# The inverse of the softmax sums moved from VectorE to GpSimd: top-k attention and a gated MLP in one kernel

## The chip, the cores and the metric

The kernel runs on one core of a Trainium2 chip. The metric is device time in microseconds. Engines are named as in the profile: PE is TensorE (PEld its weight loads), DVE is VectorE, ACT is ScalarE, POOL is GpSimd, SP is SyncE, which here issues nearly all DMAs.

## What is computed

Eight batches of eight heads, 576 rows of 64 numbers each. Of every row of scores only the 32 largest are kept; the rest get a weight of zero. Then an MLP with a sigmoid gate runs over the joined heads.

```python
scores = scale * np.matmul(q, k.transpose(0, 1, 3, 2))
kth = np.partition(scores, -top_k, axis=-1)[..., -top_k:-top_k + 1]
scores = np.where(scores >= kth, scores, -1000000000.0)
scores = scores - np.max(scores, axis=-1, keepdims=True)
attn = np.exp(scores)
attn = attn / (np.sum(attn, axis=-1, keepdims=True) + 1e-09)
x = np.matmul(attn, v)                 # heads joined: 4608 rows of 512
h = x @ w_in                           # 512 -> 2048
out = (h * (1.0 / (1.0 + np.exp(-1.702 * h)))) @ w_out
```

The change is about the division by the sum.

## The kernel before, in words

The attention is cut into 144 slots. A slot is 128 rows of scores for two heads: a tile of 128 x 2 x 576. Eighteen slots make a batch. The order of the instructions is written out by hand, slot by slot, and each engine works off its own instructions in that order.

In a slot n:

- `scores` (L328, PE) multiplies queries and keys into the only pair of score banks in PSUM.
- `copy_scores` (L339, ACT) copies them to `sc`, and `pair_up` (L349, DVE) takes the larger and the smaller of each two scores from the bank and the copy. Only then may PE write the next scores into the banks.
- `topk` (L375 MAX8 and L379 MATCH_REPLACE8, DVE) finds the 32 largest in four rounds of eight for each head, 14 steps in all.
- `bounds` (L393 `cut` and L394 `low`, POOL) makes the two bounds from the largest and the 32nd value.
- `mask` (L407, ACT) pushes scores below the cut far down, `exps` (L417, ACT) takes the exponentials into `pr` and their sum into `den`.
- `invert` (L426 or L428, and L430) adds 1e-9 to the two sums of every row (`some`) and takes their inverse (`rden`): 128 x 2 numbers.

What uses the inverse differs with the stage:

- In slots 0 to 10 (`slot`) `divide` (L437, POOL) multiplies the identity by it into two diagonals (`by`). PE turns the exponentials with these (`turn_main`, `turn_ends`, L457 and L460, one slot later), which divides them on the way; ACT copies the result to `pt` (L465). In these slots the weights are also brought in and rounded in pieces, by ACT (L155, L157, L159), DVE (L158) and POOL (L148, L151, L156). Between its other work PE runs filler products to stay warm (`stay_warm`, L174).
- From slot 11 on (`first_pair`, `filling_pair`, `steady_pair`) `normalize` (L443, POOL) multiplies the 128 x 576 exponentials of each head by it. `split` (L479, ACT) separates their 16-bit halves into `sc`, SP writes these to `rows` in DRAM (L481), and a DMA transpose brings them back as `pt` (L487). PE multiplies by the values two or three slots later (`values_at`, `values_of_two`, L546 and L575).

The inverse of slot n-1 stands in DVE's order within the top-k steps of slot n: after step 9 or 7 in `slot`, and after step 8 in `find`, which the later stages call. In the same order stands `pair_up` of the next slot, after step 9 in `slot` and after step 7 in `find`.

When four slots of 128 rows are through, their block goes into the MLP: `hidden` (L646, PE), `tanh` (L662 and a copy L665, ACT), `gate` (L674 and L675 on POOL, or L677 on DVE), `combine` (L699 to L702), `project` (L752, L737 early on, PE), and from there through `raws` (L770 ACT, L774 POOL) to the output. Around slots 13 to 18 POOL also forms differences of the weights (L722). The MLP's products fill PE between those of the attention.

Of the kernel before, what the change touches and what calls it, by code (L numbers as in the profile page):

```python
# [9 lines left out]
ALU = mybir.AluOpType  # L10
ENG = mybir.EngineType
F32 = mybir.dt.float32
# [7 lines left out]
P = 128  # L20
# [13 lines left out]
def kernel(  # L34
# [27 lines left out]
    nc = tc.nc  # L62
# [26 lines left out]
    PAIRED = SETTLED + 1  # L89
# [6 lines left out]
    const = ctx.enter_context(tc.tile_pool(name="const", bufs=1))  # L96
# [67 lines left out]
    qT, kT, vv = {}, {}, {}  # L164
    loaded = {}
    v_tail = const.tile([P, NP, 2, D], F32, name="v_e")
    for i in range(NP):
        (nc.gpsimd if i else nc.vector).memset(v_tail[:, i, :, :], 0.0)

# [143 lines left out]
    st = [{} for _ in slots]  # L313
# [108 lines left out]
    def invert(n):  # L422

        some = small.tile([P, 2], F32, name="some", tag="sums")
        if n > PAIRED:
            nc.gpsimd.tensor_scalar(some[:], st[n]["den"][:], 1e-9, None, op0=ALU.add)  # L426
        else:
            nc.vector.tensor_scalar_add(some[:], st[n]["den"][:], 1e-9)  # L428
        rden = st[n]["rden"] = small.tile([P, 2], F32, name="rden", tag="inverse")
        nc.vector.reciprocal(rden[:], some[:])  # L430

    def divide(n):

        invert(n)
        by = st[n]["by"] = diagonals[:]
        for i in range(2):
            nc.gpsimd.tensor_scalar(by[:, i, :], ident[:], st[n]["rden"][:, i : i + 1], 1.0, op0=ALU.mult, op1=ALU.mult)  # L437
# [602 lines left out]
    def find(m, at):  # L1040

        for i, op in enumerate(topk(m) if live(m) else [lambda: None] * 14):
            op()
            if i == 7 and live(m) and live(m + 1):
                pair_up(m + 1)
            if i == at and live(m - 1):
                invert(m - 1)
            if i > 1 and len(unfinished) > (2 if m == SETTLED + 1 else 0):
                finish_one()
# [214 lines left out]
```

## Time and profile before

| | |
|---|---|
| median of 3 runs | 1387.49 us (1384.41 to 1388.14) |
| span of the profiled execution | 1385.2 us |
| mean granted clock of TensorE | 0.987 |
| busy: PE, DVE, ACT, POOL | 1345.7, 1283.0, 1165.2, 963.8 us |
| reciprocal L430 on DVE | 144 times, 140/165/168 ns (min/median/max) |
| sum L426 on POOL, slots from 12 on | 132 times, 221/222/227 ns |
| sum L428 on DVE, slots before | 12 times, 168/170/1352 ns |

The profiled execution lies within the three runs; the page has no time of its own beside the span. The page of the profile tells busy times of the engines, groups of instructions by line, and the chain of work that ended last. Further views are waits (who waited for whom: us in total, number of times, longest), the instructions in order of time (start, length, engine, line; in brackets the idle time before it and what ended it), and busy times by stretch. A row with x2 joins two instructions that follow each other. Busy PE is not PE at its peak, since matmuls are pipelined and their ends are modelled.

### The profile page before, as it was taken

How to read it: one execution, taken by the hardware profiler on the slowest of the kernel's cores; microseconds unless marked ns; L12 is line 12 of the kernel's file. 1: busy time of each engine (PE TensorE's matmuls, PEld its weight loads, DVE VectorE, ACT ScalarE, POOL GpSimd, SP SyncE). 2: the span in 40 equal slices, each digit the busy share in tenths (PEclk: the TensorE clock that was granted, in tenths of full speed). 3: DMA queues.
4: the chain of work that ended last, by engine and by line, in shares of the span. 5: the costliest groups of instructions: out<-in, count | busy, mean ns of one | idle time of the engine just before them, and what ended most of it. 6: DMA issues, size and time to landing. Idle time of an engine off the chain costs nothing. (4 is left out here: it accounts for less than half of the span.)

```text
span 1385.2 us, 54404 instructions
## 1 busy us (share of the span) xinstructions
PE 1345.7 (97%) x22560; PEld 1209.1 (87%) x22560; DVE 1283.0 (93%) x3392; ACT 1165.2 (84%) x1930; POOL 963.8 (70%) x1758
## 2 busy tenths in 40 slices
PE   7889889999999999999999999999999999999998
PEld 5676568899998999999999999999999999999997
DVE  7999889999999999999999999999999999999912
ACT  6888778999998998999998998889998998888831
POOL 3777586677777777777776777777777777777770
PEclk9899999999999999999999999999999999999999
DMA  8552556988889776977798678887898878855640
GB/s 231 161 151 67 128 150 160 212 200 199 199 208 206 177 184 174 237 198 196 194 203 223 181 187 193 193 195 200 197 213 208 196 182 182 183 139 138 155 111 17
DMA packets 527223, 246.92 MB, mean 178 GB/s; under 512 B 458880, under 2 KB 505472, under 8 KB 526976
## 3 DMA queue, kind: packets, MB, share of 16 engines
q1 hardware_dynamic: 526544, 243.16, 71.7%
q8 instruction: 177, 2.90, 0.9%
q14 instruction: 70, 0.57, 0.1%
q10 hardware_dynamic: 432, 0.30, 0.1%
HBM read 46.01 MB, written 103.42 MB: 108 GB/s over the span
## 5 line engine op out<-in xcount | busy, mean ns | idle before, releaser
L375 DVE MAX8 top<-ranked 128x8 f32<-128x288 f32 (+1 forms) x1152 | 637.4, 595 | 0.0
L646 PEld LDWEIGHTS ph<-xT,win 128*64 128x64 f32 (+1 forms) x8736 | 479.7, 137 | 28.9 <-issue 25.0
L646 PE MATMUL ph<-xT,win 128*64 128x128 f32 (+1 forms) x8736 | 504.5, 273 | 0.0
L379 DVE MATCH_REPLACE8 ranked<-top,ranked 128x288 f32<-128x288 f32 (+1 forms) x864 | 462.3, 542 | 0.0
L479 ACT COPY sc<-pr 128x2304 uint16<-128x2304 uint16 x134 | 283.4, 2115 | 100.9 <-POOL pr L443 100.9
L443 POOL TENSOR_SCALAR pr<-pr,rden 128x576 f32<-128x576 f32 x268 | 198.0, 750 | 53.6 <-DVE rden L430 53.0
L417 ACT ACTIVATE pr<-sc,low 128x576 f32<-128x576 f32 x288 | 220.1, 771 | 0.0
L407 ACT ACTIVATE sc<-sc,cut 128x576 f32<-128x576 f32 x288 | 208.9, 781 | 5.6 <-POOL cut L393 5.6
L752 PE MATMUL po<-raws,h 128*64 128x128 f32 x2112 | 205.1, 273 | 0.2 <-POOL h L700 0.2
L752 PE MATMUL po<-wout,h 128*64 128x128 f32 x2112 | 205.2, 273 | 0.1
L349 DVE TENSOR_TENSOR ranked<-s_ps,sc 128x576 f32<-128x576 f32 x286 | 201.8, 747 | 0.3 <-ACT sc L339 0.3
L339 ACT COPY sc<-s_ps 128x576 f32<-128x576 f32 x286 | 168.5, 642 | 21.0 <-PE s_ps L328 13.6
L328 PE MATMUL s_ps<-qk_t 64*64 64x288 f32 x2304 | 177.5, 422 | 8.1 <-DVE ranked L349 7.7
L426 POOL TENSOR_SCALAR some<-den 128x2 f32<-128x2 f32 x132 | 29.3, 222 | 222.0 <-ACT pr L417 221.7
L675 POOL TENSOR_TENSOR th<-th,h 128x512 f32<-128x512 f32 x134 | 171.8, 1282 | 11.2
L752 PE MATMUL po<-wout,th 128*64 128x128 f32 x2176 | 165.2, 273 | 0.0
L752 PEld LDWEIGHTS po<-wout,h 128*64 128x64 f32 x2112 | 133.4, 137 | 0.6 <-POOL h L701 0.6
L752 PEld LDWEIGHTS po<-raws,h 128*64 128x64 f32 x2112 | 133.4, 137 | 0.5 <-POOL h L700 0.5
L328 PEld LDWEIGHTS s_ps<-qk_t 64*64 64x64 f32 x2304 | 76.1, 134 | 61.6 <-issue 14.4
L752 PEld LDWEIGHTS po<-wout,th 128*64 128x64 f32 x2176 | 127.7, 137 | 0.9 <-POOL low L394 0.4
L575 PE MATMUL o<-pt,v_l 128*64 128x128 f32 (+1 forms) x2240 | 124.8, 265 | 0.0
L575 PEld LDWEIGHTS o<-pt,v_l 128*64 128x64 f32 x2240 | 110.3, 137 | 10.1 <-issue 9.6
(111 smaller groups left out, 1631.3 us busy)
## 6 DMA issues: line engine op xcount, KB each, us to landing
rows<-sc SPq DMA_DIRECT2D x134, 576.0 KB, 3.8
qk_rows<-halves SPq DMA_DIRECT2D x24, 576.0 KB, 5.6
out_dram<-raws SPq DMA_DIRECT2D x68, 128.0 KB, 3.6
raws<-in_moe_w_in_dram SPq DMA_DIRECT2D x16, 512.0 KB, 4.9
raws<-in_moe_w_out_dram SPq DMA_DIRECT2D x16, 512.0 KB, 3.6
qk_l<-in_q_dram SPq DMA_DIRECT2D x28, 256.0 KB, 4.4
qk_l<-in_k_dram SPq DMA_DIRECT2D x28, 256.0 KB, 4.3
v_l<-in_v_dram SPq DMA_DIRECT2D x4, 1024.0 KB, 7.8
```

The costliest lines, as they stand in the source:

```text
L328: nc.tensor.matmul(ps[rows, i, c, 0:HALF], lhsT=qT[b, hps[p]][on, cols], rhs=kT[b, hps[p]][on, FIRST[i] + c * HALF : FIRST[i] + (c + 1) * ...
L349: nc.vector.tensor_tensor(out=ranked[n][:, :, c, :], in0=a, in1=b, op=op)
L375: nc.vector.max(top[:, i, 8 * r : 8 * r + 8], of(r, i))
L379: nc.vector.match_replace(to, top[:, i, 8 * r : 8 * r + 8], of(r, i), LOWEST)
L407: nc.scalar.activation(sc[:, i, :], sc[:, i, :], AF.Prelu, bias=cut[:, i : i + 1], scale=SCALE, alpha=HUGE)
L417: nc.scalar.activation(pr[:, i * S : (i + 1) * S], sc[:, i, :], AF.Exp, bias=low[:, i : i + 1], accum_out=den[:, i : i + 1],)
L443: nc.gpsimd.tensor_scalar(pr[:, i, :], pr[:, i, :], st[n]["rden"][:, i : i + 1], 1.0, op0=ALU.mult, op1=ALU.mult)
L479: nc.scalar.copy(out=halves, in_=pr[:].bitcast(U16).rearrange("p (k h) -> p h k", h=2))
L575: nc.tensor.matmul(o[s][j * D : (j + 1) * D, cols], lhsT=lhsT, rhs=rhs, start=(s, j) not in halves[:k], stop=(s, j) not in halves[k + 1 :],)
L646: nc.tensor.matmul(ph[rows, i * P : (i + 1) * P], lhsT=win[:, c, f * P + rows.start : f * P + rows.stop], rhs=xs[:, x.place, c, :], start= ...
L675: nc.gpsimd.tensor_tensor(out=th[:], in0=th[:], in1=h, op=ALU.mult)
L752: nc.tensor.matmul(both_banks[y * TAIL : (y + 1) * TAIL, bank, to * P : (to + 1) * P], lhsT=a[:, i, :], rhs=weight(w, fs[i])[:, y, :], sta ...
```

## The change

A constant tile of 128 x 2 with -1.0 is filled on POOL at the start. `invert` no longer uses DVE. The sum is formed on POOL in all slots, in a form with two operations (add 1e-9, multiply by 1.0), and the inverse is a POOL tensor by tensor instruction: the sum to the power of the constant. The users of `rden`, `divide` and `normalize`, stay as they were, on POOL.

```diff
+    minus_one = const.tile([P, 2], F32, name="minus_one")
+    nc.gpsimd.memset(minus_one[:], -1.0)
...
     def invert(n):
 
         some = small.tile([P, 2], F32, name="some", tag="sums")
-        if n > PAIRED:
-            nc.gpsimd.tensor_scalar(some[:], st[n]["den"][:], 1e-9, None, op0=ALU.add)
-        else:
-            nc.vector.tensor_scalar_add(some[:], st[n]["den"][:], 1e-9)
+        nc.gpsimd.tensor_scalar(some[:], st[n]["den"][:], 1e-9, 1.0, op0=ALU.add, op1=ALU.mult)
         rden = st[n]["rden"] = small.tile([P, 2], F32, name="rden", tag="inverse")
-        nc.vector.reciprocal(rden[:], some[:])
+        nc.gpsimd.tensor_tensor(out=rden[:], in0=some[:], in1=minus_one[:], op=ALU.pow)
```

## The prediction

> **What bounds the kernel now.** I read the page's busy times first (PE and DVE are both nearly full), then the busy times by stretch, then the chain that ended last, then who waits for whom.
>
> ```profile
> PE 1345.7 (97%) x22560; PEld 1209.1 (87%) x22560; DVE 1283.0 (93%) x3392; ACT 1165.2 (84%) x1930; POOL 963.8 (70%) x1758
> ```
>
> ```profile
> 300.00:1300.00 1000.00, 999.57 (x17899) 915.49 (x17895) 984.03 (x2604) 888.65 (x1439) 724.97 (x1385) 1.00 0.80 192
> 20.00:135.00 115.00, 96.08 (x852) 77.11 (x850) 108.61 (x283) 100.52 (x191) 82.95 (x102) 0.91 0.48 151
> 135.00:300.00 165.00, 154.79 (x2249) 127.00 (x2249) 151.27 (x403) 135.31 (x230) 113.72 (x190) 0.96 0.69 165
> ```
>
> After the length, the columns of a stretch are PE, weight loads, DVE, ACT and POOL busy, then the granted clock, the DMA share and GB/s. From 300 to 1300 us PE is busy 999.57 of 1000 us at a granted clock of 1.00. The chain that ended last runs through PE alone there, and the same place in the cycle of two slots comes back every 1028.56 - 1010.93 = 17.63 us:
>
> ```profile
> 1010.93 2.12 PE o L575 x40
> ...
> 1028.56 2.12 PE o L575 x40
> ```
>
> So in this stage nothing that is taken from DVE makes the kernel faster, though DVE is busy 984 of the 1000 us. Time can only be won where PE has gaps. Between 20 and 135 us (slots 1 to 10) PE has 18.9 us of them and works at a clock of 0.91; DVE is busiest there (108.6 of 115 us), ACT next (100.5). The next 165 us have 10.2 us of gaps.
>
> The waits around the inverse are, for POOL (whole span), DVE from 20 to 155 us, and DVE from 300 to 1300 us:
>
> ```profile
> POOL some L426 <- ACT pr L417: 221.7, 129, 3.4
> POOL pr L443 <- DVE rden L430: 53.0, 132, 6.2
> POOL cut L393 <- DVE top L375: 50.7, 15, 18.7
> ```
>
> ```profile
> DVE some L428 <- ACT pr L417: 10.1, 10, 3.6
> ```
>
> ```profile
> DVE rden L430 <- POOL some L426: 12.9, 32, 1.1
> ```
>
> **The change, part by part.**
>
> *The constant.* One small memset on POOL at the start. POOL's first real work, the cut of slot 0, comes after a wait of 18.7 us (the longest in the third row), so it costs nothing.
>
> *What DVE gives back in the steady stage.* 113 reciprocals of about 0.165 us and 12.9 us of waiting. PE's 999.57 us cover it: worth nothing. At the end PE goes on alone with what is finished: also nothing.
>
> *What DVE gives back in slots 1 to 12.* There both small instructions stand in DVE's own order, between two MAX8:
>
> ```profile
> L428 DVE TENSOR_SCALAR some<-den 128x2 f32<-128x2 f32 x12 | 4.8, 400 | 10.1 <-ACT pr L417 10.1
> ...
> L430 DVE RECIPROCAL rden<-some 128x2 f32<-128x2 f32 x12 | 2.0, 166 | 0.4
> ```
>
> That is 4.8 + 2.0 us of work and 10.1 us of waiting for ACT's exponentials, 16.9 us. The work includes a stall. The sum on DVE beside a POOL instruction that was running:
>
> ```profile
> 114.31 1.35 DVE L428 TENSOR_SCALAR some<-den 128x2 f32<-128x2 f32 x1 [0.36 <-ACT pr L417]
> ```
>
> ```profile
> 114.30 1.34 POOL L148 TENSOR_SCALAR raws<-raws 128x512 f16<-128x512 f32 x1
> ```
>
> Both end at 115.65: the DVE instruction lasted as long as POOL's. At DVE's usual 0.17 us the twelve would take 2.0 us, so 2.8 us of the 4.8 are such stalls, and I count them as won. The Trainium skill has a rule for it ("SBUF — State Buffer", "Who interferes with whom"): VectorE in a two-port mode and GpSimd take one pair of ports by a lock, and the later one blocks until the first has finished. The trace agrees in this pair of rows. Were it something else that holds DVE at this place, the stalls would stay and the sum below would be some 1.7 us smaller.
>
> Not all of the 16.9 us are worth time. Three waits are long:
>
> ```profile
> 68.34 0.17 DVE L428 TENSOR_SCALAR some<-den 128x2 f32<-128x2 f32 x1 [2.60 <-ACT pr L417]
> ...
> 69.95 1.40 DVE L349 TENSOR_TENSOR ranked<-s_ps,sc 128x576 f32<-128x576 f32 x2
> ```
>
> ```profile
> 103.21 0.38 DVE L428 TENSOR_SCALAR some<-den 128x2 f32<-128x2 f32 x1 [2.10 <-ACT pr L417]
> ```
>
> ```profile
> 151.75 0.17 DVE L428 TENSOR_SCALAR some<-den 128x2 f32<-128x2 f32 x1 [3.61 <-ACT pr L417]
> ```
>
> ```profile
> 68.52 1.18 ACT L339 COPY sc<-s_ps 128x576 f32<-128x576 f32 x2
> ```
>
> In the first, DVE goes on one MAX8 pair later with L349, which needs ACT's copy of the scores, and that ends at 68.52 + 1.18 = 69.70. Without the wait L349 begins at 69.7 in place of 69.95: 0.25 us won, not 2.9. ACT is late there and becomes the next wait. I count the three alike: their 8.3 us of waiting and some 1.2 us of the two instructions beside it are not won. 16.9 - 8.3 - 1.2 = 7.4 us remain, a little over 0.8 us in each of nine slots.
>
> *What POOL takes on.* It gets 144 powers of 128x2 and 12 more sums. The trace shows no power. Its nearest rows are the two dependent small instructions of the cut, and a large tensor by tensor product:
>
> ```profile
> 1029.10 0.23 POOL L393 TENSOR_SCALAR cut<-top 128x4 f32<-128x4 f32 x1
> 1029.41 0.19 POOL L394 TENSOR_TENSOR low<-cut 128x2 f32<-128x2 f32 x1
> ```
>
> ```profile
> L675 POOL TENSOR_TENSOR th<-th,h 128x512 f32<-128x512 f32 x134 | 171.8, 1282 | 11.2
> ```
>
> L394 is the same form on the same engine with another operation: 0.19 us, the lower end, since the fixed part cannot be less. The upper end that I keep is L675's 1.28 us. From these two, one more element costs (1.28 - 0.19) / 510 = 0.0021 us, so in L394 the arithmetic is almost nothing. If a power costs as much as 25 subtractions, two elements add about 0.11 us. I take **0.30 us**, near the row of the same form. The Trainium skill speaks against the move ("GPSIMD Engine Reference", "Performance versus the Vector engine"): elementwise work with two inputs takes GpSimd about twice VectorE's time. By that rule the power would take 2 x 0.165 = 0.33 us, an estimate: the sum below stays, but its margin is nearly gone, and the dear power among the rivals would be as likely as not. No row of before shows which holds for two elements.
>
> *What this does to the path den to split.* Before, in a steady slot:
>
> ```profile
> 1033.94 0.22 POOL L426 TENSOR_SCALAR some<-den 128x2 f32<-128x2 f32 x1 [1.32 <-ACT pr L417]
> 1034.46 1.48 POOL L443 TENSOR_SCALAR pr<-pr,rden 128x576 f32<-128x576 f32 x2 [0.30 <-DVE rden L430]
> ```
>
> ```profile
> 1035.97 2.11 ACT L479 COPY sc<-pr 128x2304 uint16<-128x2304 uint16 x1 [2.12 <-POOL pr L443]
> ```
>
> From sum to normalize 0.52 us. After: 0.31 from sum to power (as from L393 to L394), 0.30 for the power, 0.08 to the next dependent one (0.31 - 0.23), 0.69 us: **0.17 us later**, even without the detour over DVE. Behind it on POOL stand normalize, gate and the next cut; on ACT the split waits, and behind the split the copy of the scores, the next mask and the exponentials. ACT's waits from 300 to 1300 us say what it can bear:
>
> ```profile
> ACT sc L479 <- POOL pr L443: 80.9, 91, 2.3
> ACT xT L589 <- PE o L575: 11.9, 40, 0.4
> ACT sc L339 <- PE s_ps L328: 9.5, 28, 0.3
> ```
>
> The split waits for POOL in 91 slots. ACT's slack is what it then waits for PE, 11.9 + 9.5 = 21.4 us, or 21.4 / 91 = 0.24 us for each. A delay of 0.17 us fits, so the steady stage keeps its 17.63 us. It no longer fits from a power of 0.30 + 0.07 = **0.37 us** on. No DMA is added or moved; the ones behind the split start 0.17 us later, ahead of transposes whose blocks PE needs two slots on.
>
> *Early diagonals.* In slots 1 to 10 POOL forms the diagonals from the inverse, and in some PE waits for them:
>
> ```profile
> 93.21 3.39 PE L457 MATMUL tp<-by,pr 128*128 128x128 f32 x16 [3.48 <-POOL by L437]
> ```
>
> ```profile
> 92.15 0.66 POOL L156 TENSOR_SCALAR wout<-raws 128x512 f32<-128x512 f32 x1
> 92.78 0.73 POOL L437 TENSOR_SCALAR by<-ident,rden 128x128 f32<-128x128 f32 x2
> ```
>
> POOL came straight from L156 here, so sum and power delay the diagonals by 0.69 us, and PE and ACT with them. Two of the three slots with a long wait lie behind such a place: 1.4 us lost. Elsewhere ACT still waits for the cut and takes it up.
>
> *Sum.* 7.4 - 1.4 = 6.0 us. ACT, at 100.5 us of work in that stretch, takes over once DVE has come down from 108.6 to about 101, so I keep two thirds: **4 us**. The profiled execution would go from a span of 1385.2 to 1381.2 us. The median shown is 1387.49, 2.3 us above that span; on it, 1383.5 us.
>
> **The rivals.**
>
> *The power is dear* (ends slower). Place: ACT's split in the steady stage. It decides from 0.37 us on, and each further 0.1 us costs 91 x 0.1 = 9.1 us. At 0.50 us: 12 us lost, 3 won, 1396. At 0.80 us: 39 us lost, nothing won, 1427. At 1.28 us: 83 us, 1470. For it: nothing in the trace prices a power, and the split already waits in 91 of its slots. Against it: the small fixed price of POOL's row of the same form.
>
> *Nothing comes of DVE's time.* ACT leads in the early slots as soon as DVE is ahead, as at 68.5 us, and later diagonals eat the rest: 1387.5. For it: ACT's 100.5 us. Against it: ACT's largest wait from 20 to 155 us is for the cut, whose input is DVE's.
>
> ```profile
> ACT sc L407 <- POOL cut L393: 5.6, 6, 2.4
> ```
>
> *More than 4 us.* The slots from 13 to 21 also gain, because DVE no longer stands behind POOL's weight sums, and earlier work keeps PE's clock up: 10 us, 1377.5. Against it: POOL is the late one there, and it gets more to do.
>
> *Not what it says*: the inverse does not leave DVE, or comes out as several rows on POOL. The first is 1387.5 again, the second the dear power at 0.50 us, 1396.
>
> **How the numbers follow.** Forecast (power up to 0.37 us, early slots faster) 0.47; nothing comes of it 0.12; more than 4 us 0.06; dear power 0.33 (half of it under 0.80 us); not what it says 0.02. The range reaches from 1378 to 1427, which leaves the dearest powers and the largest gains out. The forecast's own range is 1379 to 1387, by 0 to 8 us won. A measurement of this kernel can tell about 0.3% from no change, 4.2 us, so below 1383.3 is faster: 0.06 and a little over half of the forecast, 0.33. Within: the rest of the forecast, the case of nothing, and the cheapest dear powers, 0.32. Slower 0.35.
>
> **What would show it.** The row of the power on POOL: its length, and start to start from sum to normalize (0.69). ACT's wait at the split from 300 to 1300 us: 80.9 us should rise by about 91 x 0.17 = 15 us, and its waits for PE fall by as much. PE from 300 to 1300 us still busy over 999 us. The cut of slot 10 about 4 us earlier than in this row:
>
> ```profile
> 133.70 0.22 POOL L393 TENSOR_SCALAR cut<-top 128x4 f32<-128x4 f32 x1 [2.00 <-DVE top L375]
> ```
>
> The prediction is wrong if the power lasts over 0.37 us, if PE gets gaps in the steady stage, or if the early cuts come no earlier.

## The result and the profile after

The changed kernel takes 1403.65 us (median of 4 runs, 1402.27 to 1405.25), the kernel before 1386.3 us on the same chip: a ratio of 1.0122, 95% interval 1.0095 to 1.015. It is slower by 17 us where 4 us of gain were forecast. The span of the profiled execution is 1400.5 us, 15.3 above that of before.

The page's busy times, and the busy times by stretch (columns as before):

```profile
PE 1353.8 (97%) x22560; PEld 1214.0 (87%) x22560; DVE 1278.8 (91%) x3236; ACT 1154.2 (82%) x1930; POOL 1065.5 (76%) x1915
```

```profile
20.00:135.00 115.00, 92.05 (x811) 74.74 (x809) 105.85 (x252) 95.58 (x184) 91.06 (x119) 0.90 0.49 151
135.00:300.00 165.00, 153.75 (x2228) 123.84 (x2230) 150.86 (x386) 134.20 (x227) 124.49 (x206) 0.98 0.65 159
300.00:1300.00 1000.00, 998.32 (x17727) 913.03 (x17724) 970.85 (x2466) 870.30 (x1423) 795.30 (x1485) 1.00 0.79 190
```

POOL has 102 us more to do, DVE 4 us less. In the steady stretch PE still reads as full, 998 of 1000 us, but the count beside it fell from 17899 matmuls to 17727. Both traces hold the same 22560 matmuls in all, so the pace is lost although the busy time is not; the count shows it, the share does not.

A steady slot on POOL, with the power (L427 sum, L429 power, L442 normalize), and the power's line alone (shortest, median, longest in ns):

```profile
1010.44 0.19 POOL L427 TENSOR_SCALAR some<-den 128x2 f32<-128x2 f32 x1 [1.04 <-ACT pr L419]
1010.71 0.72 POOL L429 TENSOR_TENSOR rden<-some,minus_one 128x2 f32<-128x2 f32 x1
1011.54 1.48 POOL L442 TENSOR_SCALAR pr<-pr,rden 128x576 f32<-128x576 f32 x2
```

```profile
L429 POOL TENSOR_TENSOR rden<-some,minus_one x144: 717/721/727, 25.7 to 1338.7; 128x2 f32<-128x2 f32 x144
```

The power takes 0.72 us on all 144 calls. From the sum to the normalize it is 1011.54 - 1010.44 = 1.10 us in place of 0.52: 0.58 us later in a usual slot. ACT waits for it at the split, and the waits from 300 to 1300 us (ACT's, then DVE's) show whom that reaches:

```profile
ACT sc L478 <- POOL pr L442: 132.2, 91, 2.7
ACT sc L341 <- DMA rows<-sc: 0.2, 1, 0.2
```

```profile
DVE ranked L351 <- ACT sc L341: 24.6, 56, 0.7
```

The wait at the split grew from 80.9 to 132.2 us, by 51.3 us, close to 91 x 0.58 = 53. ACT's waits for PE, 21.4 us before, are gone: PE no longer makes ACT wait, and ACT's loop through POOL sets the pace. DVE now waits for ACT's copy of the scores, which it hardly did before (0.3 us). That alone is no sign of the loss. It comes with the inverse leaving DVE: the kernel with a cheap operation in place of the power (below), which loses nothing, has it too:

```profile
DVE ranked L351 <- ACT sc L341: 23.0, 44, 2.5
```

How PE is held back can't be read from its own waits, which are 1.7 us in this stretch, all for DMA. The chain that ended last names the loop; before it ran through PE alone at this place:

```profile
1161.95 0.20 POOL some L427
...
1162.22 0.72 POOL rden L429
...
1163.78 0.76 POOL pr L442
...
1164.61 1.98 issue
1166.58 1.18 ACT sc L341 x2
...
1167.79 1.42 DVE ranked L351 x2
...
1184.43 1.18 ACT sc L341 x2
```

Sum, power, normalize, split (the 1.98 us named issue are the time of ACT's split) and copy; then, in rows left out here, the pairing and the top-k steps on DVE, ACT's next copy and exponentials, and another normalize and split. From copy to copy that is 1184.43 - 1166.58 = 17.85 us for two slots, where the kernel before takes 17.63.

Where the time was lost can be read from the starts of the cut (L393 before, L395 after) in the same slot. Slots 10, 27 and 141 of the changed kernel, and slots 27 and 141 of the kernel before:

```profile
137.70 0.23 POOL L395 TENSOR_SCALAR cut<-top 128x4 f32<-128x4 f32 x1 [2.03 <-DVE top L377]
...
300.85 0.23 POOL L395 TENSOR_SCALAR cut<-top 128x4 f32<-128x4 f32 x1
...
1318.21 0.22 POOL L395 TENSOR_SCALAR cut<-top 128x4 f32<-128x4 f32 x1
```

```profile
295.65 0.23 POOL L393 TENSOR_SCALAR cut<-top 128x4 f32<-128x4 f32 x1
...
1302.89 0.23 POOL L393 TENSOR_SCALAR cut<-top 128x4 f32<-128x4 f32 x1
```

4.0 us late in slot 10 (133.70 before), 5.2 in slot 27, 15.3 in slot 141: a third is lost at the start, two thirds slot by slot afterwards, 10.1 us in 114 slots. These are single executions. In four traces of kernels whose early slots are those of before (late half alone, two and three subtractions, power and two) the cut of slot 10 lies between 1.2 us earlier and 0.6 us later than 133.70, so the 4.0 us are clear of the scatter.

### The profile page after: what moved, and what is told of

Read it like the earlier page. It is cut to its first block, busy times and chain, and to the rows that moved or that the text cites. A ratio compares the mean times of both kernels' runs of the same rounds, so it can differ in the third digit from the quotient of the medians.

```text
span 1400.5 us, 54406 instructions
## 1 busy us (share of the span) xinstructions
PE 1353.8 (97%) x22560; PEld 1214.0 (87%) x22560; DVE 1278.8 (91%) x3236; ACT 1154.2 (82%) x1930; POOL 1065.5 (76%) x1915
## 5 line engine op out<-in xcount | busy, mean ns | idle before, releaser
L377 DVE MAX8 top<-ranked 128x8 f32<-128x288 f32 (+1 forms) x1152 | 627.9, 596 | 0.0
L442 POOL TENSOR_SCALAR pr<-pr,rden 128x576 f32<-128x576 f32 x268 | 198.2, 750 | 13.8
L674 POOL TENSOR_TENSOR th<-th,h 128x512 f32<-128x512 f32 x134 | 172.3, 1286 | 11.2
L427 POOL TENSOR_SCALAR some<-den 128x2 f32<-128x2 f32 x144 | 27.8, 193 | 179.5 <-ACT pr L419 175.5
L330 PEld LDWEIGHTS s_ps<-qk_t 64*64 64x64 f32 x2304 | 75.5, 133 | 54.5 <-issue 13.3
L574 PEld LDWEIGHTS o<-pt,v_l 128*64 128x64 f32 x2240 | 110.3, 137 | 10.1 <-issue 9.4
```

What stands on the lines that cost most here:

```text
L330: nc.tensor.matmul(ps[rows, i, c, 0:HALF], lhsT=qT[b, hps[p]][on, cols], rhs=kT[b, hps[p]][on, FIRST[i] + c * HALF : FIRST[i] + (c + 1) * ...
L377: nc.vector.max(top[:, i, 8 * r : 8 * r + 8], of(r, i))
L442: nc.gpsimd.tensor_scalar(pr[:, i, :], pr[:, i, :], st[n]["rden"][:, i : i + 1], 1.0, op0=ALU.mult, op1=ALU.mult)
L574: nc.tensor.matmul(o[s][j * D : (j + 1) * D, cols], lhsT=lhsT, rhs=rhs, start=(s, j) not in halves[:k], stop=(s, j) not in halves[k + 1 :],)
```

## The experiments

The theory: the power's time stands on the path from the exponentials' sums to their users, and counts there, in two places. In the steady stage ACT's loop through POOL becomes longer than PE's work; in the early slots the diagonals come late. The rivals: only one of the two stages loses; POOL's load counts and not the path; the power itself harms, whatever its length; and the forecast's own term, that DVE's freed time is worth 4 us. Times are medians, each beside the runs of the kernel before on the same chip.

**The early half alone, and the late half alone.**

The early half as an edit of the changed kernel (slots 0 to 11 are those up to `PAIRED`; the sum is split in the same way, and in the late half the branches are the other way round, with the early sum on DVE):

```diff
-        nc.gpsimd.tensor_tensor(out=rden[:], in0=some[:], in1=minus_one[:], op=ALU.pow)
+        if n > PAIRED:
+            nc.vector.reciprocal(rden[:], some[:])
+        else:
+            nc.gpsimd.tensor_tensor(out=rden[:], in0=some[:], in1=minus_one[:], op=ALU.pow)
```

> Sum and power on POOL in slots 0 to 11 only; from slot 12 on the sum on POOL and the reciprocal on DVE as before. Theory (the power's 0.72 us stands in the path from the exponentials' sums to their users): the cut of slot 12 comes 3 to 4 us later than before (155.64), as in the changed kernel (158.91), and stays that much behind to the end: 1389 to 1391 us. Rival 1 (all the loss is the steady stage's): no later than before, 1386 us, or 4 us earlier as the forecast had it, 1382 us.

> The other half: slots 0 to 11 as before, sum and power on POOL from slot 12 on. Theory: the slots from 27 to 141 each take 0.09 us longer (10 us together) because ACT's loop through POOL is longer than PE's work, PE runs out of slack, and the start is unchanged: 1396 to 1399 us. Rival 1 (all the loss is the steady stage's): 1402 us. Rival 2 (an early delay that is carried along): 1387 us.

Early alone 1391.67 against 1385.95 us, ratio 1.0051 (1.0035 to 1.0066). Late alone 1398.36 us, 1.0091 (1.0077 to 1.0106). So 5.7 and 12.4 us, together 18.1: the two halves add up to the whole loss, and neither rival that puts all of it in one stage holds. The early half was a little dearer than expected. In its trace the cut of slot 12 comes 3.2 us late and that of slot 141 2.9: what is lost early stays lost.

**A cheap operation in place of the power.**

```diff
-        nc.gpsimd.tensor_tensor(out=rden[:], in0=some[:], in1=minus_one[:], op=ALU.pow)
+        nc.gpsimd.tensor_tensor(out=rden[:], in0=some[:], in1=minus_one[:], op=ALU.subtract)
```

> The changed kernel with a subtraction in place of the power, everything else equal; the inverse is left out, so the weights are not divided. The subtraction should take 0.19 us in place of 0.72, the normalize begin 0.54 us after the sum (before 0.52, changed kernel 1.10). Theory: the steady stage is PE's again with a period of 17.63 us per two slots. What the early slots then give is the forecast's other term: if DVE's freed time is worth the 4 us of the forecast, 1382 us; if ACT and POOL take over at once, 1386 to 1388 us. Rival (the number of POOL instructions or leaving DVE costs, not the power's length): 1396 us or more.

1385.72 us (12 runs) against 1385.95 (17 runs), ratio 1.0000 (0.9989 to 1.0011). A slot of this kernel on POOL:

```profile
1003.05 0.19 POOL L427 TENSOR_SCALAR some<-den 128x2 f32<-128x2 f32 x1 [2.24 <-ACT pr L419]
1003.32 0.20 POOL L429 TENSOR_TENSOR rden<-some,minus_one 128x2 f32<-128x2 f32 x1
1003.62 1.47 POOL L442 TENSOR_SCALAR pr<-pr,rden 128x576 f32<-128x576 f32 x2
```

0.57 us from sum to normalize, and the whole loss is gone. That fits the theory. It also speaks against the forecast's gain: with everything as in the changed kernel but the price of the power, nothing is won (the interval leaves room for 1.5 us). The span of the profiled execution of this kernel, 1380.9 us, would have suggested 4 us of gain. It was the fastest of its twelve runs; the runs of either kernel spread over 6 to 7 us, so only the repeated times decide here.

**The sums alone.**

```diff
-        if n > PAIRED:
-            ...
+        nc.gpsimd.tensor_scalar(some[:], st[n]["den"][:], 1e-9, 1.0, op0=ALU.add, op1=ALU.mult)
         nc.vector.reciprocal(rden[:], some[:])
```

> The sum on POOL in all slots, in the new form with two operations, the reciprocal on DVE as before. It tells what moving the early sums alone does: theory: the sum of slots 0 to 11 now stands behind POOL's rounding instructions, DVE waits for it in its own order, so the early cuts come later by up to 1 us a slot where POOL is busy: 1386 to 1392 us. Rival (DVE only gains, 0.17 us and the stalls beside POOL): 1383 us.

1399.05 us, ratio 1.0100 (1.0085 to 1.0115): dearer than expected, and all of it early. The cut of slot 10 comes 11.1 us late, and what follows loses nothing more. DVE's waits from 20 to 160 us name the cause:

```profile
DVE rden L427 <- POOL some L425: 22.5, 10, 2.8
```

POOL's sum stands behind its rounding steps, and DVE, with its own work queued behind the reciprocal, waits. In the kernel with the subtraction the early sums are on POOL too and nothing is lost; there the inverse has left DVE as well, and it waits for neither.

**How long may the path be?** Two, then three chained subtractions from slot 12 on, and the power with two subtractions behind it; slots 0 to 11 as before. The inverse is left out or spoilt in these.

```diff
+        if n > PAIRED:
+            for i in range(2):          # or 3; or the power first, then 2 of rden
+                nc.gpsimd.tensor_tensor(out=rden[:], in0=rden[:] if i else some[:],
+                                        in1=minus_one[:], op=ALU.subtract)
```

> Slots 0 to 11 as before; from slot 12 on two chained subtractions on POOL in place of the power (the inverse is left out there). From the sum to the normalize 0.87 us in place of 0.52 before and 1.10 with the power: 0.35 us later than before. Theory (one delay for each two slots stands in the loop that binds, which has 0.39 us of slack: 0.58 less the 0.19 us by which two slots grew): just inside the slack, period still 17.63 us, 1386 to 1388 us. Rival 1 (no slack, each delay counts in proportion): 0.35/0.58 of the 12 us of the late half, 1393 us. Rival 2 (the power itself harms, not the time it takes): 1386 us.

> Slots 0 to 11 as before; from slot 12 on three chained subtractions in place of the power: the same time from sum to normalize as with the power (1.13 us against 1.10), and nearly the same POOL time, without a power. Theory (the time on the path counts): 1398 to 1401 us, as the late half alone (1398). Rival (the power itself harms, for instance by holding a port against DVE): 1386 us.

> Slots 0 to 11 as before; from slot 12 on the power and two subtractions behind it (what is divided by is no inverse). From sum to normalize 1.70 us, 1.18 later than before. It tells how many delays of each two slots count. Theory, one of two: period 17.63 + 1.18 - 0.39 = 18.42 us, about 50 us in 64 pairs, 1436 us. Rival 1 of the prediction's count, 1.6 of two (91 waits in 57 pairs): 1.18 x 1.6 less a slack of 0.75 that fits the changed kernel, 1.14 us a pair, 1459 us. Rival 2, both count: 1.18 x 2 - 0.97 = 1.39 us a pair, 1475 us.

| from slot 12 on | sum to normalize, us | later than before, us | ratio (95% interval) | loss by medians, us |
|---|---|---|---|---|
| one subtraction (in all slots) | 0.57 | 0.05 | 1.0000 (0.9989 to 1.0011) | 0 |
| two subtractions | 0.85 | 0.33 | 1.0000 (0.9991 to 1.0009) | 1 |
| the power | 1.10 | 0.58 | 1.0091 (1.0077 to 1.0106) | 12 |
| three subtractions | 1.12 | 0.60 | 1.0093 (1.0080 to 1.0105) | 13 |
| the power and two subtractions | 1.65 | 1.13 | 1.0557 (1.0538 to 1.0576) | 79 |

The three subtractions and the power with two of them, start to start:

```profile
1010.33 0.19 POOL L428 TENSOR_SCALAR some<-den 128x2 f32<-128x2 f32 x1 [1.05 <-ACT pr L419]
1010.60 0.19 POOL L434 TENSOR_TENSOR rden<-some,minus_one 128x2 f32<-128x2 f32 x1
1010.88 0.47 POOL L434 TENSOR_TENSOR rden<-rden,minus_one 128x2 f32<-128x2 f32 x2
1011.45 0.74 POOL L449 TENSOR_SCALAR pr<-pr,rden 128x576 f32<-128x576 f32 x1
```

```profile
1007.99 0.19 POOL L428 TENSOR_SCALAR some<-den 128x2 f32<-128x2 f32 x1
1008.27 0.72 POOL L433 TENSOR_TENSOR rden<-some,minus_one 128x2 f32<-128x2 f32 x1
1009.07 0.47 POOL L435 TENSOR_TENSOR rden<-rden,minus_one 128x2 f32<-128x2 f32 x2
1009.64 0.75 POOL L450 TENSOR_SCALAR pr<-pr,rden 128x576 f32<-128x576 f32 x1
```

Three subtractions that take as long as the power cost as much as the power: it is the time on the path, not the kind of operation. The cost has a threshold between 0.33 and 0.58 us. From 0.58 to 1.13 us of delay the loss grows by 67 us, 122 us for each us; carried back along a straight line, it begins at 0.58 - 12.4 / 122 = 0.48 us, an estimate from two kernels. There are 132 slots from slot 12 on, so at 122 us for each us nearly every slot's delay counts. The theory of one delay in two (1436 us expected) fell: 1465.03 us lies between the rivals with 1.6 of two (1459) and with both (1475).

**POOL's load beside the path.** A power that nobody reads, behind the instructions that use the inverse: in all slots, then behind the diagonals only. The trace has ten such powers: diagonals are formed for the inverses of slots 0 to 9, and slot 10 is normalized already.

```diff
+        nc.gpsimd.tensor_tensor(out=aside[:], in0=st[n]["some"][:], in1=minus_one[:], op=ALU.pow)
```

> The kernel before, with a power of the same size added on POOL behind the instructions that use the inverse (diagonals in slots 0 to 10, normalize later); nobody reads it. POOL has the same extra work as in the changed kernel, but the path from the sum to the split is as before. Theory (time on the path counts, not POOL's work): 1386 to 1389 us, the little more because the gate and the next cut stand behind it. Rival (POOL's load counts): as the changed kernel or more, 1400 us.

> The kernel before, with an unread power on POOL right behind the two diagonals in slots 0 to 10 only. The diagonals come as before, but POOL's rounding steps behind them and the next cut come up to 0.83 us later. If only the lateness of the diagonals makes the early half's loss: 1386 to 1387 us. If POOL's queue as such counts there: 1390 us, as the early half alone (1391).

All slots: 1391.28 against 1385.74 us, ratio 1.0033 (1.0021 to 1.0045), above the theory's 1386 to 1389 and far below the rival's 1400. Early only: 1386.77 against 1384.81 us, 1.0015 (1.0006 to 1.0024). The same POOL work off the path costs some 2 us early (0.8 to 3.3 by the interval), in place of the early half's 5.7, and from then on about 0.0018 or 2.5 us, in place of 12.4; this difference of two ratios is uncertain by some 2 us. So most of the late loss is the path's, and some 60% of the early one. The rest would be POOL's queue, if the two costs simply add, which no run tests.

**What DVE's time is worth at most.** Slots 0 to 9 without sum and inverse; the diagonals take the sum itself, the division is left out there. The sums and inverses of slots 10 and 11 stay on DVE.

```diff
     def divide(n):
-        invert(n)
+        st[n]["rden"] = st[n]["den"]
```

> Slots 0 to 10 without sum and inverse: the diagonals take the sum of the exponentials itself (the division is left out there). DVE gets all its time back, and POOL has nothing more to do: the most that freeing DVE can give. If DVE binds the early slots as the forecast said: 6 us, 1380 us. If ACT and POOL take over at once: 1384 to 1386 us.

1385.64 against 1385.74 us (12 and 23 runs), ratio 0.9998 (0.9986 to 1.0009). DVE is freed and POOL not charged, and nothing is won; the interval leaves room for 2 us. The waits from 20 to 160 us:

```profile
PE tp L460 <- ACT pt L465: 7.6, 6, 3.6
...
DVE ranked L349 <- ACT sc L339: 5.5, 5, 2.4
```

In five slots DVE now stands at the pairing and waits for ACT's copy of the scores; PE waits longer for ACT too (4.7 us before for the first row). In all, DVE waits 11.2 us there (5.5 at the pairing, 4.3 at the two sums that are left, 1.4 for a tanh), where it waited 10.1 before. DVE had been the busiest engine, but what it no longer waits for at the inverse it waits for elsewhere.

**The diagonals earlier.** On POOL, ahead of the rounding step L156 that stands in front of them in slots 3 to 10; once in the kernel before, once with the early half of the change.

```diff
-                if last and n > 2:
-                    last["pool_size"]()
...
                     divide(n - 1)
-                if last and n < 3:
+                if last:
                     last["pool_size"]()
```

> The kernel before, and in slots 3 to 10 the diagonals are formed on POOL ahead of the rounding step of 0.66 us (L156) that stood in front of them. If the late diagonals bind the early slots (PE waits 5.9 us for them from 20 to 135 us), they come up to 0.66 us earlier in four or five slots: 2 to 3 us faster, 1383 us. If POOL's whole queue binds, or something else: no change, 1386 us.

> The early half alone (sum and power on POOL in slots 0 to 11), and the diagonals ahead of the rounding step L156. With the power they came 0.8 us later; the other order gives 0.66 us back. If the diagonals' lateness makes the early half's 5.7 us: most of it goes, 1387 us. If it is that POOL's work before the next cut grows by the power, whatever the order: 1391 us.

In the kernel before: 1386.70 against 1387.15 us, ratio 1.0003 (0.9994 to 1.0012), no change. Its trace doesn't show that PE gained by the new order: from 20 to 160 us PE waits 7.1 us for the diagonals, 5.9 before. With the early half: 1390.57 us, 1.0025 (1.0013 to 1.0036) in place of 1.0051, and PE's wait for the diagonals is 5.2 us in place of 7.9. So delayed by the power the diagonals bind, and forming them ahead of the rounding step takes back about half.

What the other half is stays open. One cause that no run separates is DVE's own rounding steps (L158). They last longer with the early half on POOL. Before, then in the changed kernel (16 instructions each, busy us and mean ns):

```profile
L158 DVE TENSOR_SCALAR win<-win 128x512 uint32<-128x512 uint32 x16 | 7.5, 519 | 0.0
L158 DVE TENSOR_SCALAR wout<-wout 128x512 uint32<-128x512 uint32 x16 | 5.8, 414 | 0.0
```

```profile
L158 DVE TENSOR_SCALAR win<-win 128x512 uint32<-128x512 uint32 x16 | 12.0, 801 | 0.0
L158 DVE TENSOR_SCALAR wout<-wout 128x512 uint32<-128x512 uint32 x16 | 7.2, 501 | 0.0
```

That is 13.3 and 19.2 us. With the early half alone it is 18.9 us, in either order of the diagonals, with the subtraction 16.1, with the early unread powers 15.7, and 13.1 to 13.3 in the four kernels whose early slots are those of before. No version tried here beats the kernel before.

## Why the prediction was wrong, step by step

*The price of the power* is the step that failed first: 0.30 us taken, 0.72 measured. The estimate of 25 subtractions for each element had nothing under it; if the excess is spent by element, which one shape can't tell, (0.72 - 0.19) / 2 = 0.27 us for each is some 125 of them. The row of the same form priced a subtraction, and said nothing about the arithmetic of another operation. The rule of the Trainium skill that was set beside it ("GPSIMD Engine Reference", "Performance versus the Vector engine"), about twice VectorE's time, which it measured on an add of 2048 numbers a row, does not carry over to this operation either: 0.72 against 0.165 us is 4.4 times. With 0.72 us the prediction's own rival, the dear power, was the case that came about, with the place it named, ACT's split.

*The rival's price* was too high: 0.72 us would have given 91 x 0.35 = 32 us, and the late half lost 12.4. Its slope was not the fault (91 us for each us; about 120 from the two kernels), the point where it begins was: 0.24 us of delay forecast, about 0.48 by the straight line above, which is a power of about 0.62 and not 0.37 us. That it lies above 0.33 us, the two subtractions show without a line. The slack was read from ACT's waits for PE alone. ACT's waits for DMA and DVE in the same stretch, another 7 us, vanished almost wholly as well, which makes (21.4 + 7) / 91 = 0.31 us. What the rest is was not settled.

*The steady stage is PE's* held for before and for every delay up to 0.33 us. That PE would stay busy for over 999 of 1000 us as the sign of it was a poor test: it reads 998.3 in the changed kernel and 999.5 with the late half alone, which loses 12 us, but 998.4 with the two subtractions, which lose nothing.

*DVE's early time is worth 4 us* is the second step that failed. The two instructions and their waits left DVE as reckoned, and no gain is measured: at most 2 us by the interval without early sums and inverses. The rival "nothing comes of DVE's time" was right on this term. The prediction saw ACT as the next wait in three slots and kept nine others; without the inverses DVE waits for ACT's copy in five slots, and as long in all as before. That ACT takes over in every slot is not shown. In that trace the cut of slot 10 comes 2.1 us earlier, not 4, and that is little more than the 1.2 us which a kernel with an unchanged early half shows. The 2.8 us of stalls beside POOL that were counted as won came back elsewhere on DVE: its rounding steps (L158) take 5.9 us more in the changed kernel, and 2.1 us more (15.4 us) even without the early sums and inverses.

*Early diagonals* were rightly named and too small: 1.4 us forecast, where the early half as a whole lost 5.7 and the other order of the diagonals took back about half. The delay from sum to diagonals is 1.10 us and not 0.69, and POOL's queue behind them is late as well. PE's waits for the diagonals from 20 to 160 us, before and after:

```profile
PE tp L457 <- POOL by L437: 5.9, 5, 3.5
```

```profile
PE tp L456 <- POOL by L436: 8.1, 5, 3.1
```

In the same slot that the prediction showed (93.21 there), PE and POOL of the changed kernel:

```profile
96.98 3.52 PE L456 MATMUL tp<-by,pr 128*128 128x128 f32 x16 [3.06 <-POOL by L436]
```

```profile
95.46 0.19 POOL L427 TENSOR_SCALAR some<-den 128x2 f32<-128x2 f32 x1
95.73 0.72 POOL L429 TENSOR_TENSOR rden<-some,minus_one 128x2 f32<-128x2 f32 x1
96.56 0.73 POOL L436 TENSOR_SCALAR by<-ident,rden 128x128 f32<-128x128 f32 x2
```

The power stands in POOL's order directly ahead of the diagonals that PE is waiting for. In this one slot PE's wait is no longer than before (3.06 and 3.48 us); the whole slot is 3.8 us late by then.

*The constant and the unchanged DMAs* cost nothing, as said; the kernel with the subtraction has them too.

## What to carry to other kernels

An operation that the trace of before does not show has no price from its neighbours of the same shape; until one run measures it, the forecast should hang on the two prices between which the sign turns. A hop to another engine that costs 0.3 us, with the instruction there, can be cheaper than staying on an engine whose instruction is slow: what counts on a path is the time from start to start, not the number of engines. And waiting on the busiest engine is worth something only if what it would do next is ready; look at the first instruction behind the wait and at who feeds it.

## What the runs showed of the hardware beyond that

A power of 128 x 2 on GpSimd takes 0.72 us on every one of 144 calls (0.717 to 0.727 us), the first like the last, where a subtraction of the same form takes 0.195 us. Each further small dependent instruction on GpSimd costs about 0.28 us from start to start (1010.60 to 1010.88), of which 0.19 are its own. The sum in the form with two operations (add, then multiply by 1.0) is the shorter one: with the early half alone, where one trace holds both, it takes 0.191 us on 12 calls, and with one operation 0.220 us on 132.
